# Strassen's seven products in the down projection of a transformer block, from the second super chunk on

## The chip, the cores and the metric

The kernel runs on one core of a Trainium2 chip. The core has TensorE (PE, matrix products into PSUM banks), VectorE (DVE), ScalarE (ACT) and GpSimd (POOL) for element-wise work, and SyncE (SP), which here only issues DMA transfers. Each engine works through its own list of instructions in order; semaphores tie the lists together. The metric is the device time of one execution in microseconds (us), the median of several runs. Before the change it is 2608.47 us (three runs, 2606.03 to 2609.94).

## What is computed

A transformer block on one sequence of 2048 tokens, width 576, all in float32:

```python
h  = x + attention(layernorm(x), wqkv, wo)      # 32 heads of 18
g  = layernorm(h) @ w_gate                      # 576 x 4608
u  = layernorm(h) @ w_up                        # 576 x 4608
h2 = h + (gelu(g) * u) @ w_down                 # 4608 x 576
```

The change touches the last line only: the product with `w_down` (the down product) and how its left factor, gelu(g) * u, is handed over.

## The kernel before

Float32 accuracy comes from pairs of float16: each factor is cut into a high part and a low part (value less high part), and a product of two factors is three float16 matmuls (high x high, high x low, low x high) added up in PSUM.

The feed-forward part runs from about 1392 us to the end. The 4608 hidden columns are cut into 18 chunks `c` of 256, two chunks make a super chunk `sc` (nine in all). The tokens are cut into four blocks of 512, two blocks make a pair `p`. For one super chunk the order of work is: unit(c, 0) and unit(c+1, 0), down(0), unit(c, 1) and unit(c+1, 1), down(1). The down product of pair 0 of super chunk `sc+1` stands at the end of the loop body of `sc` (L1364 to L1391).

**unit(c, p)** (L1111 to L1200) makes gelu(g) * u for 256 hidden columns and 1024 tokens. Gate and up products are done by a Strassen scheme in seven products each, so that a unit has 14 products of seven matmuls (L1125). The products go by turns into six PSUM banks, `g[0..2]` and `u[0..2]`. A bank is used several times in a unit: the first, fifth, ninth and eleventh product all add into `g[0]` (the second, sixth, tenth and twelfth into `u[0]`), and between two of them ACT copies the sum so far into a temporary (L1143, L1158, L1171 for `g[0]`; L1146, L1162, L1175 for `u[0]`). DVE adds the other banks to the temporaries (L1149, L1153, L1172, L1177, L1192, L1196), ACT applies gelu (L1130), DVE multiplies by u (`gate`, L1133). The result is four blocks of 128 hidden columns by 512 tokens, made one after the other in the temporaries xg, bg, ga and ag. Each is cut: `high` is a cast to float16 on ACT (L1136), `low` is a subtraction on POOL (L1139). The last one, ag, is ready only after the fourteenth product: addition L1196, gate L1133, high, low.

**down(p, dsc)** (L1202 to L1219) multiplies the result with `w_down`: eight row blocks of 128 tokens, two column halves of 288, each a group of 12 matmuls of 128x288 (four hidden blocks of 128, three matmuls each; issued from L300) in one of four banks. DVE multiplies a finished bank with the scale and adds it to `nat`, the residual rows in SBUF (L1215). `nat` holds all 2048 rows (16 tiles of 576 columns) throughout; after the last super chunk the rows are stored to the output (L1219).

**Side work.** Weights for the next super chunk are prepared beside these products, in steps: a generator yields after each step, and `take` runs one step of it after a product of the main work. What a step issues stands in the engines' lists at that place. `split_matrix` (L982 to L1035) is one such generator, made four times a super chunk: g2, u2, g3, u3 (gate and up matrices of the next two chunks). It makes four block sums on POOL (L993), takes the largest magnitude (`exponents`, L129 to L146: DVE reductions, a small transpose on PE, a few small DVE operations), and then cuts the matrix, in three steps each with an ACT high part (L1013) and two DVE low parts (L1027, L1029). With its `then` it has the next matrix loaded over SP (L977, L979). `split_down` (L1080 to L1105) is the last: two reductions, the small chain that gives the scale `p_s_dn`, and then four pieces, ACT high (L1096, L1100) and DVE low (L1101), into `dh` and `dl`. The order of the side steps is written in the driver:

```python
side = chain(g2, pause(2), u2, pause(2), g3, pause(2), u3, pause(4), dn)
beside(islice(u := unit(c + 1, 1), 13), side)
run(u)
beside(down(1, dsc, last), side, head=2)
```

`beside` takes one side step after each product of the main work (after `head` of them). The lists of PE, DVE, ACT, POOL and SP all have the written order (`manual_schedule`).

## Time and profile before

| what | value |
|---|---|
| runs | 2606.03, 2608.47, 2609.94 us; median 2608.47 |
| profiled execution, span | 2604.1 us |
| TensorE busy | 2579.3 us, 99% |
| DVE / ACT / POOL busy | 2010.0 / 1661.3 / 818.9 us |
| down products (L300, 128x288) | 3456 matmuls |
| unit products (L1125, 128x512) | 3528 matmuls |
| moved by DMA | 118.23 MB |

The profile is of one execution. Its page gives each engine's busy time, groups of equal instructions with their count, total and mean time, and the idle time before them with what ended it. The chain of waits goes back from the last instruction to what released each step: what stands on it sets the end. A timeline lists single instructions: start, length, engine, line, operation, tile written <- tiles read, and in brackets the idle time before it. A view by windows gives each engine's busy time within a stretch: PE, weight loads, DVE, ACT, POOL, then the granted clock. Names such as `p_s_m` are the program's tiles; `bank` and `more` are PSUM banks. For matmuls the length of one contains its way through the array, so the pace is read from the starts.

### The profile page before, as it was taken

The page shows a single profiled execution, that of the slowest core. Times are in us where ns is not written, and L with a number is a line of the kernel's source. Part 1 is how long each engine was busy: PE and PEld are TensorE (multiplying, and loading weights), DVE is VectorE, ACT ScalarE, POOL GpSimd, SP SyncE. Part 2 cuts the span into 40 slices and gives each one's busy share as a digit, 9 for nine tenths or more (in the row PEclk, how much of TensorE's full clock was granted, in tenths as well). Part 3 has the DMA queues.
Part 4 walks back from the last instruction along what each step waited for, and adds up shares of the span by engine and source line. Part 5 has one row for each costly group of instructions (what it writes and reads, how often), then busy time and mean ns, then how long its engine had stood idle before and what let it go on. Part 6 is the DMA issues. An engine that isn't in the chain of part 4 may idle for free.

```text
span 2604.1 us, 53642 instructions
## 1 busy us (share of the span) xinstructions
PE 2579.3 (99%) x20765; PEld 1198.2 (46%) x20765; DVE 2010.0 (77%) x3886; ACT 1661.3 (64%) x3124; POOL 818.9 (31%) x1146
## 2 busy tenths in 40 slices
PE   8999999999999999999999999999999999999999
PEld 4543333333333333333335555555555555555555
DVE  8479999999999999999867675757565656565653
ACT  6229999999999999999774543424243433333332
POOL 4302532322223232324585432323232323222221
PEclk9999999999999999999999999999999999999999
DMA  8621010101001010101135410101010101010110
GB/s 227 154 77 45 17 47 17 44 19 39 20 23 41 16 43 16 47 16 32 38 64 116 83 34 30 34 30 34 30 34 30 34 30 34 30 34 30 34 56 37
DMA packets 170193, 118.23 MB, mean 45 GB/s; under 512 B 88664, under 2 KB 147564, under 8 KB 169938
## 3 DMA queue, kind: packets, MB, share of 16 engines
q1 hardware_dynamic: 161198, 98.47, 14.2%
q0 software_dynamic: 8608, 16.33, 2.6%
q8 instruction: 162, 2.65, 0.4%
q14 instruction: 93, 0.76, 0.1%
q10 hardware_dynamic: 132, 0.01, 0.0%
HBM read 80.05 MB, written 15.01 MB: 37 GB/s over the span
## 4 chain that ended last, share of the span: by engine, by line
PE 92%; DVE 4%; POOL 1%; DMA 1%; issue 1%; ACT 1%; SPq 0%; POOLq 0%; ACTq 0%
PE bank L673 19%; PE bank L1125 15%; PE more L1125 15%; PE bank L300 11%; PE more L300 8%; PE quad L615 7%; PE bank L615 6%; PE quad L300 4%; PE quad L665 4%; DVE mx L625 3%; PE bank L665 3%; DVE nat L688 1%; DMA A<-qk_hi 0%; POOL A L1055 0%; ACT A L155 0%
## 5 line engine op out<-in xcount | busy, mean ns | idle before, releaser
L667 ACT ACTIVATE WK<-quad 128x512 f32<-128x512 f32 x1170 | 656.2, 621 | 23.4 <-PE quad L665 21.0
L673 PE MATMUL bank<-WK,V 128*32 128x256 f32 x8192 | 606.6, 388 | 2.7 <-DVE nat L688 0.6
L625 DVE TENSOR_REDUCE mx<-quad 128x1 f32<-128x512 f32 x836 | 553.8, 684 | 9.0 <-PE quad L665 1.5
L667 ACT ACTIVATE WK<-bank 128x512 f32<-128x512 f32 x878 | 504.9, 622 | 11.1 <-PE bank L665 9.3
L625 DVE TENSOR_REDUCE mx<-bank 128x1 f32<-128x512 f32 x716 | 477.1, 684 | 33.5 <-PE bank L615 26.4
L300 PEld LDWEIGHTS <-WK 128*128 128x128 f16 x3456 | 338.2, 98 | 88.3
L1125 PEld LDWEIGHTS <-W 128*128 128x128 f16 x2394 | 234.3, 98 | 278.3
L673 PEld LDWEIGHTS bank<-WK,V 128*32 128x32 f32 x8192 | 190.0, 108 | 268.2 <-issue 201.3
L300 PE MATMUL more<-W,WK 128*128 128x288 f16 x1728 | 235.2, 286 | 0.0
L300 PE MATMUL bank<-W,WK 128*128 128x288 f16 x1728 | 235.2, 286 | 0.0
L698 POOL TENSOR_TENSOR rp<-rc,minus_one 128x4 f32<-128x4 f32 x112 | 111.2, 1012 | 383.9 <-DMA rc<-nat 383.9
L1125 PE MATMUL bank<-X,W 128*128 128x512 f16 x792 | 223.8, 379 | 0.0
L1125 PE MATMUL bank<-V,W 128*128 128x512 f16 x720 | 202.4, 379 | 0.0
L993 POOL TENSOR_TENSOR A<-A 128x384 f32<-128x384 f32 x136 | 138.1, 1036 | 200.2 <-DMA A<-in_B_w_up_dram 83.7
L615 PE MATMUL quad<-W 54*128 54x512 f16 x514 | 191.0, 382 | 0.2 <-DVE mx L625 0.2
L615 PEld LDWEIGHTS <-W 54*128 54x128 f16 x1024 | 74.5, 94 | 241.3 <-issue 226.8
L1139 POOL TENSOR_TENSOR WK<-tmp,WK 128x512 f16<-128x512 f32 x73 | 88.5, 1212 | 305.8 <-ACT WK L1136 305.6
L615 PEld LDWEIGHTS <-A 54*128 54x128 f16 x1024 | 71.1, 94 | 231.0 <-issue 216.7
L1143 ACT COPY tmp<-more 128x512 f32<-128x512 f32 x36 | 20.9, 582 | 238.3 <-PE more L1125 203.4
L665 PE MATMUL quad<-A 56*128 56x512 f16 x584 | 172.1, 380 | 0.3
L615 PE MATMUL quad<-A 54*128 54x512 f16 x462 | 171.6, 382 | 0.1
L665 PE MATMUL quad<-W 56*128 56x512 f16 x586 | 167.5, 380 | 0.1
(348 smaller groups left out, 4122.3 us busy)
## 6 DMA issues: line engine op xcount, KB each, us to landing
A<-in_B_w_down_dram SPq DMA_DIRECT2D x8, 1152.0 KB
nat<-rc SPq DMA_DIRECT2D x32, 256.0 KB
A<-in_B_w_gate_dram SPq DMA_DIRECT2D x64, 128.0 KB
A<-in_B_w_up_dram SPq DMA_DIRECT2D x64, 128.0 KB
qk_hi<-tmp SPq DMA_DIRECT2D x36, 128.0 KB
qk_lo<-tmp SPq DMA_DIRECT2D x36, 128.0 KB
out_dram<-nat SPq DMA_DIRECT2D x16, 288.0 KB
X<-nat SPq DMA_DIRECT2D x100, 36.0 KB
```

Of the source, the lines that this page charges most:

```text
L300: nc.tensor.matmul(dst, a, b, start=(i == 0), stop=(i == len(pairs) - 1))
L615: nc.tensor.matmul(pm[:, :TB], Q[r, q0 : q0 + P], keys, start=True, stop=True)
L625: nc.vector.tensor_reduce(dst, pm[:, :TB], axis=AX.X, op=ALU.max)
L665: nc.tensor.matmul(pS[:, :TB], K[r, kt * P : (kt + 1) * P], Q[r, qc * TB : (qc + 1) * TB], start=True, stop=True)
L667: nc.scalar.activation(pes[(2 * kt + hh // 2) % NPE][:, hh % 2], pS[:, :TB], AF.Exp, scale=ex_reg)
L673: nc.tensor.matmul(acc[32 * hh : 32 * hh + 32, qs], Vg[n // NB][:, kt * G4 + hh * VC : kt * G4 + hh * VC + 32], pes[(2 * kt + hh // 2) % N ...
L688: (nc.scalar.copy if n >= NS - 2 else nc.vector.tensor_copy)(oT, acc[:, :TB])
L698: nc.gpsimd.tensor_tensor(rc[:, c : c + 4], den[:, c : c + 4], minus_one.to_broadcast([P, 4]), op=ALU.pow)
L993: op(W8[:, d], W8[:, a], W8[:, b])
L1125: nc.tensor.matmul(bank, w, x_, start=start and i == 0, stop=i == len(mm) - 1, skip_group_check=not start)
L1139: nc.gpsimd.tensor_sub(hl[:, 2 * i + j], v, hh[:, 2 * i + j])
L1143: nc.scalar.copy(xg, g[0])
```

## The change

From the second super chunk on, the down product of one super chunk and one pair, a 2 x 2 block product (two hidden halves, two blocks of tokens against two column halves), is done by Strassen's scheme with seven block products in place of eight. This needs sums of the factors:

- `unit`, for c >= 2, makes seven left factors in place of four: A11 (bg), A12 (ag), A22 (xg), and HS1 = ga + xg, HS2 = HS1 - bg, HS3 = bg - ga, HS4 = ag - HS2. The sums are four added DVE operations; seven highs on ACT and seven lows on POOL take the place of four each. Five of the seven lows now stand at the end of the unit.
- `split_down7` takes the place of `split_down`: it scales `w_down` on ACT in place (two 128x1152), forms four sums on POOL (128x576), and cuts seven parts, each an ACT copy and a DVE subtraction (128x576). The POOL memset of `blank_rows` ends it, as before.
- `down7` takes the place of `down`: for two row tiles at a time seven products of six matmuls, two of them at a time by turns in six banks, which are the banks of `unit`. Three of the seven add on to the sum that a former one left in its bank, after DVE has added that sum to the rows. DVE has 24 additions of 128x288 and 4 of twice 288 in a call. In `down7(1)` a side step is taken after every second product, from the third on.
- The seven right factors lie where `nat` had the rows of pair 1. So only one pair's rows are in SBUF: as rows are done they are stored to `nat_d` in DRAM (in the last super chunk to the output), and after the products the other pair's rows are loaded. The first super chunk keeps `down` and stores pair 1's rows.
- One temporary moves and one is added; pause(4) becomes pause(2); scale constants change.

The core of the diff:

```diff
+    def split_down7(sc):
+        df = view(A, W8O, (4, D))
+        ed = yield from exponents([view(A, W8O + 4 * 2 * D * i, (1, 2 * D)) for i in range(2)], "dn")
+        s = down_scale(ed, 266, -258)
+        B11, B12 = (df[:, 1::2, n * HALF : (n + 1) * HALF] for n in range(2))
+        B21, B22 = (df[:, ::2, n * HALF : (n + 1) * HALF] for n in range(2))
+        T3 = view(A, W8O + 4 * 4 * D, (2, HALF))
+        def part(m, v):
+            h, l = (d[:, m].rearrange("p (c n) -> p c n", c=2) for d in (dh7, dl7))
+            nc.scalar.copy(h, v)
+            nc.vector.tensor_sub(l, v, h)
+        for c in range(2):
+            nc.scalar.activation(df[:, 2 * c : 2 * c + 2], df[:, 2 * c : 2 * c + 2], AF.Copy,
+                                 scale=s[:, c : c + 1])
+        nc.gpsimd.tensor_sub(T3, B22, B12)
+        nc.gpsimd.tensor_sub(B12, B12, B11)
+        yield
+        part(HA11, B11)
+        part(HA12, B21)
+        yield
+        nc.gpsimd.tensor_sub(B11, B22, B12)
+        nc.gpsimd.tensor_sub(B21, B21, B11)
+        part(HS4, B22)
+        part(HS1, B12)
+        yield
+        part(HS3, T3)
+        part(HS2, B11)
+        yield
+        part(HA22, B21)
+        blank_rows()
+        yield
...
         gate(ga, u[0])
-        high(1, 0, ga)
-        low(1, 0, ga)
+        if seven:
+            nc.vector.tensor_add(xu, ga, xg)
...
         gelu(ag, ag)
+        if seven:
+            high(HS1, xu)
+            low(HS1, xu)
+            nc.vector.tensor_sub(bu, xu, bg)
...
         gate(ag, au)
+        if seven:
+            high(HS2, bu)
+            low(HS2, bu)
+        high(A12_, ag)
+        low(A12_, ag)
+        if seven:
+            nc.vector.tensor_sub(ga, bg, ga)
+            nc.vector.tensor_sub(au, ag, bu)
+            high(HS3, ga)
+            low(HS3, ga)
+            high(HS4, au)
+            low(HS4, au)
...
+    def down7(p, dsc, last, more):
+        Xs, Bs, Zs = ([banks[k], banks[3 + k]] for k in (1, 0, 2))
...
+        def leave(t):
+            g = 2 * p * TPB + t
+            nc.sync.dma_start(ov[:, g] if last else nat_d[:, g], nat[:, t])
+        for i0 in range(0, TPB, 2):
+            for m, bs, start, n in ((HA11, Xs, True, 0), (HA22, Bs, True, 0), (HS1, Zs, True, 1),
+                                    (HS2, Xs, False, 1), (HA12, Bs, True, 0), (HS3, Xs, False, None),
+                                    (HS4, Zs, False, 1)):
+                for k in range(2):
+                    i = i0 + k
+                    product(bs[k], m, i, start)
+                    if m == HS3:
+                        add2(bs[k], i)
+                        leave(i)
+                    else:
+                        add(bs[k], i if m in (HA22, HS1) else TPB + i, n)
+                        if m == HS4:
+                            leave(TPB + i)
+                    yield
+        if more:
+            for t in range(2 * TPB):
+                nc.sync.dma_start(nat[:, t], nat_d[:, 2 * (1 - p) * TPB + t])
...
-            side = chain(g2, pause(2), u2, pause(2), g3, pause(2), u3, pause(4), dn)
+            side = chain(g2, pause(2), u2, pause(2), g3, pause(2), u3, pause(2), dn)
...
-        beside(down(1, dsc, last), side, head=2)
+        if sc:
+            for i, _ in enumerate(down7(1, dsc, last, not last)):
+                if i >= 2 and i % 2 == 0:
+                    take(side)
+        else:
+            beside(down(1, dsc), side, head=2)
+            tmps[5] = view(nat1, 15 * 4 * D, (TB,))
+            tmps.append(view(V, 36864, (TB,)))
...
-        beside(down(0, dscs[-1], sc == NCH // 2 - 2), iter(()))
+        run(down7(0, dscs[-1], sc == NCH // 2 - 2, True))
```

More of the change, by code (lines that the diff above doesn't have):

```diff
@@ new lines, in tile_block @@
+    DT = 2 * HALF
+    dh7 = view(nat1, 8 * 4 * D, (7, DT), F16)
+    dl7 = view(nat1, 8 * 4 * D + 2 * 7 * DT, (7, DT), F16)
+    HA11, HA12, HS4, HA22, HS1, HS2, HS3 = range(7)
+    h7 = [([view(WK, 2 * TB * m, (TB,), F16) for m in range(7)],
+           [view(WK, 2 * TB * (7 + m), (TB,), F16) for m in range(7)]),
+          ([view(W, 23296 + 2 * TB * m, (TB,)) for m in range(7)],
+           [view(W, 23296 + 2 * TB * (7 + m), (TB,)) for m in range(5)]
+           + [view(WK, 2 * TB * (14 + m), (TB,), F16) for m in range(2)])]
@@ L1203, in down @@
+    def down(p, dsc):
         for j in range(2):
@@ L1359, in tile_block @@
     run(side)
-    for i, _ in enumerate(down(0, dscs[-1], NCH == 2)):
+    for i, _ in enumerate(down(0, dscs[-1])):
         take(rows, 1 + (i % 4 == 3))
```

80 lines of the change are left out of this document (52 added, 28 removed).

## Prediction

> **What bounds the kernel now.** I read the page first, then the chain of waits over the feed-forward stage, then the chain of one super chunk, and last the timelines of DVE, ACT and POOL there.
>
> ```profile
> span 2604.1 us, 53642 instructions
> PE 2579.3 (99%) x20765; PEld 1198.2 (46%) x20765; DVE 2010.0 (77%) x3886; ACT 1661.3 (64%) x3124; POOL 818.9 (31%) x1146
> ```
>
> The chain of waits from 1700 us to the end:
>
> ```profile
> by line: PE bank L1125 31.4%; PE more L1125 31.3%; PE bank L300 18.2%; PE more L300 18.2%; PE more L138 0.2%; PE bank L138 0.2%; DVE nat L1215 0.1%; issue 0.0%
> ```
>
> In this stage the set end is TensorE alone: it never waits. A matmul removed there is time saved, and any wait put there is time lost. The same chain, one super chunk (start, length, what):
>
> ```profile
> 2092.91 1.51 PE more L1125 x7
> ...
> 2114.28 1.47 PE more L300 x12
> ```
>
> A unit is fourteen products of 1.51 us (with two small transposes in this one, 21.37 us to the next start), a down call sixteen groups of 1.47 us, without a gap.
>
> **What is removed.** A down call has 16 x 12 = 192 matmuls; the new one has 4 x 7 = 28 products of 6 = 168, of the same shape. One matmul is 1.47 / 12 = 0.1225 us, a product of six 0.735 us. Saved: 24 x 0.1225 = 2.94 us a call, in 16 of the 18 calls: 47.0 us. If nothing waits, the span is 2557.1 us. Per super chunk the saving is 5.9 us, and I look for the waits that eat it: TensorE, ACT, DVE and POOL each work in written order, so a step put ahead of an operation delays it.
>
> **What hides.** Rows leave and return through SP: eight stores and eight loads of 288 KB (2.36 MB each way) a call. The next call that needs them is two units (42 us) away.
>
> ```profile
> 2090.65 0.37 SPq L1075 DMA_DIRECT2D A<-in_B_w_down_dram  x1
> ```
> ```profile
> 2095.93 2.61 DVE L129 TENSOR_REDUCE ac_dn<-A 128x1 f32<-128x1152 f32 x2 [1.43 <-DMA A<-in_B_w_down_dram]
> ```
>
> 1152 KB issued at 2090.65 were read at 2095.93, 5.3 us later, so 4.7 MB take about 22 us. SP also issues the matrix loads; those behind the row loads come half a unit later or more. I take nothing; without that cover it would be some 11 us a call for the loads. The temporaries that move, the scale constants and the shorter pause cost nothing by themselves.
>
> **Price list.** Durations of the nearest operations:
>
> ```profile
> L711 POOL TENSOR_TENSOR nat<-nat 128x512 f32<-128x512 f32 x30 | 38.3, 1276 | 189.9 <-DMA nat<-rc 119.8 <-DVE mx L625 55.3 <-DVE mx L623 7.4
> L1139 POOL TENSOR_TENSOR WK<-WK 128x512 f16<-128x512 f32 x35 | 40.5, 1157 | 96.1 <-ACT WK L1136 96.1
> L909 POOL TENSOR_TENSOR A<-A 128x288 f32<-128x288 f32 x4 | 3.2, 805 | 11.3 <-ACT A L907 11.3
> ```
> ```profile
> L248 ACT CAST A<-nat 128x576 f16<-128x576 f32 x16 | 10.0, 671 | 5.7 <-DVE nat L236 4.6 <-issue 1.0
> L1013 ACT ACTIVATE W<-A,p_s_m 128x1152 f16<-128x1152 f32 x26 | 32.6, 1255 | 119.8 <-DVE p_s_m L173 119.8
> L1175 ACT COPY tmp<-bank 128x512 f32<-128x512 f32 x35 | 20.5, 585 | 19.4 <-PE bank L1125 18.6
> ```
> ```profile
> L851 DVE TENSOR_TENSOR V<-V 128x512 f16<-128x512 f32 x2 | 1.4, 694 | 0.1
> ```
>
> From 288 to 512 columns POOL adds 0.47 us, so a 576-column subtraction is 1.4 us (an estimate; at one rate per column it would be 1.44). A `low` is 1.16 us, a part's ACT copy 0.67, a DVE subtraction 0.65.
>
> DVE and POOL also hold each other up:
>
> ```profile
> 1418.05 1.75 DVE L1027 SCALAR_TENSOR_TENSOR W<-A,p_s_m,W 128x768 f16<-128x768 f32 x1
> 1419.84 1.40 DVE L1029 SCALAR_TENSOR_TENSOR W<-A,p_s_m,W 32x384 f16<-32x384 f32 x1
> ```
> ```profile
> 1416.58 2.41 POOL L993 TENSOR_TENSOR A<-A 128x384 f32<-128x384 f32 x2
> 1418.96 1.87 POOL L1139 TENSOR_TENSOR WK<-tmp,WK 128x512 f16<-128x512 f32 x1
> ```
>
> The next rows have L1027 at 1.02 and L1029 at 0.61 undisturbed; here they took 0.73 and 0.79 more, and POOL's 1.16 became 1.87: they take turns, one whole operation each. The tail of a new unit is just such a queue: five `low`s on POOL against gate and two subtractions on DVE.
>
> **Wait A: the unit before `down7(0)`, 8 times.** `split_down7` lies there as side steps. The 26 side steps taken up to the end of `down7(1)` (13 and 13) are g2's four, a pause of two, u2's nine, two, g3's nine; the next unit takes 14: two, u3's nine, two, the first of `split_down7`. So in the unit after it the sixth step, with the scalings, stands behind the fifth product, and the seventh to ninth, a pair of parts each (last HS3 and HS2), behind the sixth to eighth: ahead of ACT's copy of the ninth product (L1171). The eleventh product adds into that bank and must wait for that copy. Today:
>
> ```profile
> 2093.75 0.75 DVE L1133 SCALAR_TENSOR_TENSOR WK<-W,p_hsc,WK 128x512 f32<-128x512 f32 x1
> ...
> 2100.81 0.42 DVE L142 TENSOR_REDUCE ab_dn<-bank 128x2 f32<-128x256 f32 x1
> ...
> 2101.92 1.01 DVE L1089 TENSOR_TENSOR M<-e_dn 128x1 int32<-128x1 int32 x1
> ...
> 2103.77 0.17 DVE L173 TENSOR_SCALAR p_s_dn<-pi_s_dn 128x2 int32<-128x2 int32 x1
> ```
> ```profile
> 2103.98 0.78 ACT L1096 ACTIVATE W<-A,p_s_dn 128x576 f16<-128x576 f32 x1 [1.16 <-DVE p_s_dn L173]
> ```
>
> The scale p_s_dn is ready at P = 11.1 us after the unit's start at 2092.91, and TensorE waits for nothing that ACT does there (the chain above). In the new kernel, from P: two scalings on ACT 2.4; then POOL T3 1.4, B12 1.4, the unit's own `low` 1.16, B11 1.4, so P + 7.8; HS2's copy 0.67 and the delayed copy 0.58: P + 9.0. The eleventh product is due at 10 x 1.51 + 0.2 = 15.3. With P = 11.1, 4.9 us are lost. But P moves: DVE ended the unit ahead at 1.5 (2093.75 + 0.75); to that come u3's last cut, now one product later (1.2, as the two rows of 2054.82 below), and four subtractions (2.6), less 0.6 that falls into gaps: 4.7. Its two-input operations take turns there with three `low`s, up to 1.16 each: 7.9. Then two reductions 2.6, two additions and a gate 2.0, the small chain 2.3 (2100.81 to 2103.94 less L1089's 0.85 of waiting), 0.2 for gelu: P = 15.0. Loss 24.0 - 15.3 = 8.7; without the turns P = 11.8 and 5.5. I take the first, since the rows at 1416 us are this very pattern. A wait of 3 us at the fifth product (ACT copies HS4 ahead of the first bank) is contained in it. 8 x 8.7 = 69.6.
>
> **Wait B: `down7(1)` with the side work, 7 times.** The tail and the additions today, in the down call that began at 2048.02:
>
> ```profile
> 2048.20 1.02 DVE L1027 SCALAR_TENSOR_TENSOR WK<-A,p_s_m,W 128x768 f16<-128x768 f32 x1 [0.73 <-ACT W L1013]
> 2049.24 0.61 DVE L1029 SCALAR_TENSOR_TENSOR W<-A,p_s_m,W 32x384 f16<-32x384 f32 x1
> 2049.89 0.69 DVE L1196 TENSOR_TENSOR W<-bank,W 128x512 f32<-128x512 f32 x1
> 2050.68 0.75 DVE L1133 SCALAR_TENSOR_TENSOR WK<-W,p_hsc,WK 128x512 f32<-128x512 f32 x1
> 2051.35 0.51 DVE L1215 SCALAR_TENSOR_TENSOR nat<-more,p_dsc,nat 128x288 f32<-128x288 f32 x1
> 2051.78 0.51 DVE L1215 SCALAR_TENSOR_TENSOR nat<-bank,p_dsc,nat 128x288 f32<-128x288 f32 x1
> ...
> 2054.82 0.74 DVE L1027 SCALAR_TENSOR_TENSOR WK<-A,p_s_m,W 128x512 f16<-128x512 f32 x1
> 2055.58 0.47 DVE L1029 SCALAR_TENSOR_TENSOR W<-A,p_s_m,W 32x256 f16<-32x256 f32 x1
> ...
> 2058.79 0.94 DVE L129 TENSOR_REDUCE ac_m<-A 128x1 f32<-128x768 f32 x1
> ```
> ```profile
> 2047.90:2071.50 23.60, 23.60 (x195) 18.88 (x194) 17.47 (x34) 6.06 (x8) 5.06 (x5) 1.00 0.13 37
> ```
>
> DVE (third busy number) already has 17.5 of 23.6 us there. An addition follows the last after 0.43 to 0.44 us. Instead of 16 there are 24 of 0.44 and 4 double ones of 0.74 (0.3 for 288 columns more): 13.5 us, in a call of 20.7. The first could start at 3.3 us today (2051.35 less 2048.02); at 5.3 with three more subtractions ahead that don't fall into the wait for ACT; at 8.4 if three `low`s take turns (3.1). HS2 adds into HA11's bank and is due at 3 x 1.47 = 4.4, so TensorE waits at once. The queue then stays behind it. Up to the first half's second double addition DVE has ten additions 4.4, two double ones 1.5, u2's last two cuts 2.4 with a `low` to wait for 1.0, the scales 0.6 (four of 0.15) and a reduction 0.95: 8.4 + 10.85 = 19.3. That addition frees the bank of the second half's second product, and TensorE has 13 products of 0.735 left from there, and a transpose of 0.1: end at 29.0 instead of 20.7. Behind it DVE's lag no longer reaches TensorE (HS2's second addition stands at 25.8, its bank is due at 26.8). Without turns: 5.3 + 9.85 = 15.2, end at 24.8. Loss 8.3; 4.1 without. 7 x 8.3 = 58.1.
>
> **Wait C: plain tails.** Before `down7(0)` gate ends at 1.5, then `low` 1.16, subtraction 0.65, `low`, subtraction: 5.1, first addition 5.5 against 4.4: 1.1, eight times, and once in the last call: 9.9. Between the units of pair 1 ACT's HS4 copy and bank copy end at 6.3 against 6.04: 0.3 x 8 = 2.4. Without turns, nothing.
>
> **Sum.** -47.0 + 69.6 + 58.1 + 9.9 + 2.4 = +93.0: span 2697.1. The median of the runs is 2608.47 - 2604.1 = 4.4 above the span, so 2701.5 us.
>
> One place more: the window above shows a granted clock of 1.00 (the number behind POOL's), and TensorE has no gap there, so the sum makes no matmul slower. By the Trainium skill, "TensorE: Matmul & The Clock Gate", Part 1, an idle window of about 3.4 us halves TensorE's clock until a busy one has passed; wait A has a gap of some 4.5 us, so an estimate by that page is one gap in three holding a whole window, each costing 2 to 3 us: 5 to 8 us more, 2707 to 2710. No row here shows such a gap; at even odds it stays inside the forecast's case.
>
> **Rivals.**
> 1. The waits come, but POOL's turns cost DVE little, because the `low`s are late themselves: A 4.9 to 5.5, B 4.1, C nothing. -47 + 8 x 5.5 + 7 x 4.1 = +26 (2634); with P = 11.1 +21 (2629). For it: no L1215 row was stretched, and turns are rare today. Against it: L1027 and L1029 above.
> 2. Faster: ACT's queue doesn't hold the eleventh product. That needs the copy by 15.3, so P + 9.0 <= 15.3 or parts that run behind the copy. With B spread by the side's gaps too, 2561; with A at P = 9.9 (the fourth product ends at 6.2, addition, gate and small chain 3.7, nothing late) and no B, -47 + 8 x 3.6 = -18: 2590. The point at which it decides is 5.9 us of waiting a super chunk. Against it: ACT alone has 7.0 us from P to the copy, and P can't precede the fourth product.
> 3. The interleaved views of one buffer are held to overlap, so that ACT's parts wait for POOL's in-place sums one after the other: the copy at about P + 13.5, 4.5 us more in A, 8 x 4.5 = 36: 2737. Nothing in this trace shows such views.
>
> **Chances.** Forecast 0.48, rival 1 0.24, rival 2 0.14, rival 3 or longer 0.09; 0.05 that waits and saving meet within 0.2% (5 us, about what a measurement of this kernel can tell from no change). Slower 0.81, same 0.05, faster 0.14. Range 2600 to 2745: it leaves out rival 2 and a few in a hundred above rival 3. For the slower cases alone 2629 to 2737.
>
> **What would show it.** TensorE's share falls from 99% to about 95%, with 384 matmuls fewer. The waits should name ACT's copy of the ninth product before a unit product (about 8 of them, 4 to 5 us each) and `nat` additions before `down7` products. In `down7(1)` DVE should be busy throughout, with HS2 and HS3 products starting late; `down7(0)` should take about 21.7 us, `down7(1)` about 29. Wrong: if the stage shows TensorE with no waits (then rival 2), if the wait sits on rows landing from DRAM, or if DVE's subtractions stay at 0.7 beside POOL's `low`s (then rival 1).

## The result and the profile after

The changed kernel takes 2758.32 us (median of four runs, 2754.67 to 2758.85), the kernel before 2608.88 (four runs): a ratio of 1.0572, 95% interval 1.0559 to 1.0585. It is 149.4 us slower; 93.0 were forecast, and 2758 lies 13 us above the range.

The page of the changed kernel:

```profile
span 2757.0 us, 54241 instructions
...
PE 2594.8 (94%) x20381; PEld 1174.7 (43%) x20381; DVE 2321.2 (84%) x4230; ACT 1740.0 (63%) x3260; POOL 1034.9 (38%) x1274
```

The 384 matmuls are gone (20765 to 20381), and TensorE's share fell from 99% to 94%. DVE has 311 us more, POOL 216 more. The chain of waits over the same stretch as before, from 1700 us to the end:

```profile
by line: PE more L1175 14.9%; PE bank L1175 13.5%; PE more L1286 10.2%; PE bank L1286 10.0%; issue 9.1%; DMA A<-in_B_w_up_dram 2.1%; DVE tmp L1183 2.1%; DVE W L1029 2.1%; DVE nat L1291 1.9%; DVE W L1027 1.7%; DVE V L1183 1.7%; DVE tmp L1267
```

TensorE held all but 1% of this chain before; now its two kinds of product (L1175 units, L1286 `down7`) hold 49%, and DVE's lines stand among them. ("issue" is time in which an engine waited for nothing that the profile shows; the view breaks the line off at its end.) What TensorE waited for in the feed-forward stage, from 1390 us (sum, times, longest):

```profile
PE more L1286 <- DVE nat L1291: 48.6, 23, 3.1
PE more L138 <- DVE am_dn L133: 20.7, 4, 5.2
PE bank L138 <- DVE am_dn L133: 19.8, 4, 5.2
PE more L1175 <- ACT nat L1226: 16.9, 4, 5.9
PE more L1175 <- ACT tmp L1226: 14.2, 4, 4.2
PE more L1175 <- ACT V L1198: 4.3, 8, 0.5
```

Line 1 is the additions of `down7`, lines 4 and 5 ACT's copy of the ninth product: both were forecast. Lines 2 and 3 were not forecast: the transposes of `w_down`'s maxima stand in TensorE's list, and TensorE stops at them.

From the starts of TensorE's stages in both traces, summed over all super chunks in which the scheme runs:

| stage | times | before, us | forecast change | measured change |
|---|---|---|---|---|
| unit pair ahead of `down7(0)` | 8 | 341.0 | +69.6 | +109.2 |
| `down7(0)` | 8 | 188.2 | -23.5 + 8.8 = -14.7 | -5.9 |
| unit pair ahead of `down7(1)` | 8 | 339.9 | +2.4 | +14.3 |
| `down7(1)` with side work | 7 | 165.4 | -20.6 + 58.1 = +37.5 | +31.6 |
| the last `down7(1)`, to the end of the span | 1 | 27.3 | -2.9 + 1.1 = -1.8 | -0.8 |
| sum (of the unrounded times) | | | +93.0 | +148.2 |

The other 4.6 us of the difference of the spans (152.8) lie ahead of the first of these stages, which began that much later in this execution.

**One unit ahead of `down7(0)`.** It starts at 2175.03 and takes 34.44 us instead of 21.37. TensorE:

```profile
2179.56 1.68 PE L1175 MATMUL bank<-X,W 128*128 128x512 f16 x7
2186.41 0.69 PE L138 MATMUL bank<-id,am_dn 128*128 128x128 f32 x2 [5.18 <-DVE am_dn L133]
2186.89 3.19 PE L1175 MATMUL more<-V,W 128*128 128x512 f16 x7
2189.88 2.66 PE L1175 MATMUL bank<-V,W 128*128 128x512 f16 x7
...
2201.75 2.83 PE L1175 MATMUL more<-V,W 128*128 128x512 f16 x7 [3.16 <-ACT nat L1226]
2204.36 2.25 PE L1175 MATMUL bank<-V,W 128*128 128x512 f16 x7
```

Two stops, in brackets, and behind each the next two products take 3.0 and 2.5, or 2.6 and 2.1 us from start to start, where 1.51 is usual. DVE at the tail of the unit ahead, and the parts:

```profile
2178.78 1.74 DVE L1183 SCALAR_TENSOR_TENSOR WK<-nat,p_hsc,WK 128x512 f32<-128x512 f32 x1
2180.45 1.64 DVE L1266 TENSOR_TENSOR tmp<-A,tmp 128x512 f32<-128x512 f32 x1
2182.01 1.64 DVE L1267 TENSOR_TENSOR nat<-WK,V 128x512 f32<-128x512 f32 x1
2183.57 2.60 DVE L129 TENSOR_REDUCE ac_dn<-A 128x1 f32<-128x1152 f32 x2
...
2190.66 0.17 DVE L173 TENSOR_SCALAR p_s_dn<-pi_s_dn 128x2 int32<-128x2 int32 x1
2194.66 9.01 DVE L1133 TENSOR_TENSOR nat<-A,nat 128x576 f16<-128x576 f32 x6 [3.82 <-ACT nat L1132]
```

The gate and the two subtractions take turns with POOL's `low`s (1.6 to 1.7 us each), as forecast. The scale is ready at 2190.83, P = 15.8 (forecast 15.0). POOL's sums and the unit's own `low` behind it, and the end of ACT's line:

```profile
2193.71 1.41 POOL L1138 TENSOR_TENSOR A<-A 128x576 f32<-128x576 f32 x1 [7.94 <-issue]
2195.20 1.80 POOL L1139 TENSOR_TENSOR A<-A 128x576 f32<-128x576 f32 x1
2196.97 1.67 POOL L1194 TENSOR_TENSOR W<-tmp,W 128x512 f16<-128x512 f32 x1
2198.60 1.91 POOL L1144 TENSOR_TENSOR A<-A 128x576 f32<-128x576 f32 x1
```
```profile
2200.54 0.67 ACT L1132 CAST nat<-A 128x576 f16<-128x576 f32 x1 [2.26 <-POOL A L1144]
2201.12 0.58 ACT L1226 COPY nat<-more 128x512 f32<-128x512 f32 x1
```

The copy ends at 2201.70, P + 10.9, where P + 9.0 was forecast.

**One `down7(1)`**, from 2125.54: DVE's tail and first addition, TensorE's two long stops, and the window of the stage.

```profile
2130.13 1.64 DVE L1266 TENSOR_TENSOR tmp<-V,tmp 128x512 f32<-128x512 f32 x1
2131.69 1.64 DVE L1267 TENSOR_TENSOR A<-nat,tmp 128x512 f32<-128x512 f32 x1
2133.26 0.51 DVE L1291 SCALAR_TENSOR_TENSOR nat<-more,p_dsc,nat 128x288 f32<-128x288 f32 x1
```
```profile
2133.81 0.88 PE L1286 MATMUL more<-nat,WK 128*128 128x288 f16 x3 [3.08 <-DVE nat L1291]
2140.43 0.53 PE L1286 MATMUL more<-nat,WK 128*128 128x288 f16 x3 [1.85 <-DVE nat L1291]
```
```profile
2125.54:2153.77 28.23, 22.85 (x171) 17.21 (x170) 26.81 (x48) 9.32 (x12) 11.71 (x10) 0.94 0.20 69
```

The first addition starts 7.7 us in (forecast 8.4), HS2 stops for it, HS3 stops later; DVE is busy for 26.8 of 28.2 us, and the stage lasts 28.2 (forecast 29.0).

### The profile page after: what moved, and what is told of

The parts are those of the page before. It is cut to its first block, busy times and chain, and to the rows that moved or that the text cites. A ratio compares the mean times of both kernels' runs of the same rounds, so it can differ in the third digit from the quotient of the medians.

```text
span 2757.0 us, 54241 instructions
## 1 busy us (share of the span) xinstructions
PE 2594.8 (94%) x20381; PEld 1174.7 (43%) x20381; DVE 2321.2 (84%) x4230; ACT 1740.0 (63%) x3260; POOL 1034.9 (38%) x1274
## 3 DMA queue, kind: packets, MB, share of 16 engines
q1 hardware_dynamic: 195758, 169.27, 20.6%
## 4 chain that ended last, share of the span: by engine, by line
PE 70%; DVE 16%; issue 5%; ACT 3%; DMA 2%; POOL 2%; SPq 1%; DVEq 0%; ACTq 0%; POOLq 0%
PE bank L673 18%; PE more L1175 8%; PE bank L1175 7%; PE quad L615 7%; PE bank L615 6%; PE more L1286 4%; PE bank L1286 4%; PE quad L300 4%; PE quad L665 4%; PE bank L300 4%; PE bank L665 3%; DVE mx L625 3%; PE more L300 1%; DMA A<-in_B_w_up_dram 1%; DVE W L1029 1%
## 5 line engine op out<-in xcount | busy, mean ns | idle before, releaser
L667 ACT ACTIVATE WK<-quad 128x512 f32<-128x512 f32 x1170 | 656.3, 621 | 26.0 <-PE quad L665 23.6
L625 DVE TENSOR_REDUCE mx<-bank 128x1 f32<-128x512 f32 x716 | 477.3, 685 | 35.5 <-PE bank L615 26.8
L1175 PEld LDWEIGHTS <-W 128*128 128x128 f16 x2394 | 242.6, 101 | 341.4 <-issue 85.5
L1175 PE MATMUL bank<-X,W 128*128 128x512 f16 x792 | 225.3, 382 | 0.0
L1175 PE MATMUL bank<-V,W 128*128 128x512 f16 x720 | 212.3, 395 | 0.5 <-ACT WK L1217 0.5
L1286 PEld LDWEIGHTS <-WK 128*128 128x128 f16 x1472 | 147.3, 100 | 97.1 <-issue 54.2
L1286 PE MATMUL more<-nat,WK 128*128 128x288 f16 x736 | 142.4, 294 | 48.6 <-DVE nat L1291 48.6
L1013 ACT ACTIVATE W<-A,p_s_m 128x768 f16<-128x768 f32 (+1 forms) x78 | 79.0, 1036 | 149.1 <-DVE p_s_m L173 149.1
L1175 PE MATMUL more<-V,W 128*128 128x512 f16 x414 | 125.3, 439 | 36.0 <-ACT nat L1226 16.9
L615 PE MATMUL bank<-A 54*128 54x512 f16 x442 | 152.3, 383 | 1.9 <-DMA A<-qk_hi 1.8
```

What stands on the lines that cost most here:

```text
L615: nc.tensor.matmul(pm[:, :TB], Q[r, q0 : q0 + P], keys, start=True, stop=True)
L625: nc.vector.tensor_reduce(dst, pm[:, :TB], axis=AX.X, op=ALU.max)
L667: nc.scalar.activation(pes[(2 * kt + hh // 2) % NPE][:, hh % 2], pS[:, :TB], AF.Exp, scale=ex_reg)
L1013: by = hi_on or (lambda dst, src, k: nc.scalar.activation(dst, src, AF.Copy, scale=k))
L1175: nc.tensor.matmul(bank, w, x_, start=start and i == 0, stop=i == len(mm) - 1, skip_group_check=not start)
L1286: nc.tensor.matmul(bank[:, :HALF], a, b, start=start and k == 0, stop=k == len(mm) - 1, skip_group_check=not start)
```

## The experiments

Stage times below are means over the super chunks from the third on unless said otherwise (the other pair without the last one, `down7(1)` over its seven calls with side work); "pair" is the unit pair ahead of `down7(0)`. Each experiment was run twice; a trace is of one execution. In the changed kernel: pair 56.0, `down7(0)` 22.9, other pair 44.4, `down7(1)` 28.1; before: 42.6, 23.5, 42.5, 23.6.

**1. Without the tail's lows.** Theory 1 was that of the prediction: turns of DVE and POOL, and ACT's line. Theory 2: the rows that go to DRAM and back.

```diff
             high(HS1, xu)
-            low(HS1, xu)
+            if c < 4:
+                low(HS1, xu)
```

(and so for HS2, A12, HS3 and HS4.)

> Leaves out the five low subtractions at the end of a unit (HS1, HS2, HA12, HS3, HS4) from the third super chunk on, so POOL has nothing to do there; the low parts used are those of the second super chunk. Theory 1 (the queues: turns of DVE and POOL in the tail, ACT held behind the parts, DVE overfull in down7(1)): down7(1) from 28.1 to about 24.8 us in six calls (-20), down7(0) from 22.6 to 20.7 in seven (-13), the units of pair 0 some 4 to 5 us shorter a super chunk (-32), those of pair 1 1 us (-7): 2686 us. Theory 2 (the residual rows' way through DRAM holds up the weight loads, and those the rest): no change, 2750 to 2765.

2693.9 us, 8 above what theory 1 gave: the pair fell by 2.8 us (to 52.3 to 53.9) where 4 to 5 were expected. Further, `down7(0)` fell to 20.6 to 21.2, the other pair to 42.5, `down7(1)` to 25.0 to 25.3 but for one of 26.7. Five POOL operations a unit are worth 64 us, though POOL is busy for less than half of the time: the two subtractions at the end of the unit (L1266, L1267) fall from a median of 1.64 us to 0.68. Waits of TensorE for a `low` itself were only 3.4 us in the changed kernel. Rival 1 ("turns cost DVE little") falls. Without the lows the scheme is still 85 us slower than before.

**2. Without the rows' traffic.**

```diff
-            nc.sync.dma_start(ov[:, g] if last else nat_d[:, g], nat[:, t])
+            if last:
+                nc.sync.dma_start(ov[:, g], nat[:, t])
...
-                nc.sync.dma_start(nat[:, t], nat_d[:, 2 * (1 - p) * TPB + t])
```

> Leaves out the stores of residual rows to DRAM between super chunks and their loads (71 MB), so the sums of the two pairs run together; all else as after. Theory 1 (queues): 2750 to 2762 us, every stage as long as before. Theory 2 (row traffic): most of the 149 us comes back, 2620 to 2690.

2760.7: nothing. Theory 2 falls, and the prediction's nothing for the transfers was right.

**3. `split_down7` three products later.**

```diff
-            side = chain(g2, pause(2), u2, pause(2), g3, pause(2), u3, pause(2), dn)
+            side = chain(g2, pause(2), u2, pause(2), g3, pause(2), u3, pause(5), dn)
```

> The pause ahead of the down matrix's preparation is 5 steps in place of 2, nothing else: the transposes stand behind the seventh product in place of the fourth, the parts behind ACT's copy of the ninth product. Theory 1: TensorE's wait of 5.2 us at the transposes goes, the wait for the copy shrinks to some 3 to 4 us; a unit pair of pair 0 from 55.7 to about 47 us, in all 2680 to 2700 us. Theory 2 (row traffic): no change by more than 10 us.

2744.4, a miss by 44. The pair lost 6.6 us (to 49.4) and the stop at the transposes was gone, but two others came up. In the pair the fifth product now stops for 3.6 us (for ACT's copy of the first bank, L1198), which the prediction had named as contained in wait A. And `down7(0)` grew by 5.6 to 28.5, where TensorE now waited for parts (DVE L1133, 2.9 us each time) and for lows. The stop had only moved: the parts had no room behind them.

**4. TensorE kept busy in its gaps.** Idle matmuls ahead of the transposes (14), of the eleventh product (9), and of the first HS2 of `down7(1)` (9).

```diff
+            fill_pe(14)
         pt = next(m_ring)
...
+        if seven and p == 0 and c % 2:
+            fill_pe(9)
         product(0, g[0], A22, T4, False)
```

> After, with idle matmuls of 128x512 in TensorE's queue ahead of its long waits (14 before the down matrix's transposes, 9 before the eleventh product there, 9 before HS2's first product in down7(1)): they add nothing to what is waited for, but shorten the gaps to about 2 us. If the matmuls after a gap are slow because the gap is long (clock halved), they come back to full pace: 1.7 us in a unit of pair 0 and 1.4 us in down7(1), 8 x 1.7 + 7 x 1.4 = 23: 2735 us. If their slowness has another cause, 2758 or a little more.

2759.4. The pair lost 1.6 us (to 54.1 to 54.3, once 55.4), with a granted clock of 0.97 where it was 0.91. `down7(1)` stayed at 28.1 to 28.2 in three cases and took 29.6 to 31.1 in four, for a cause that was not looked for, so nothing was won in all. The slow pace is on the path in the pair. In `down7(1)` it costs nothing: in the changed kernel the call that began at 2427.92 had the same stop of 3.07 us at HS2, but a granted clock of 1.00, and took 28.1 us like the others (28.0 to 28.2 at 0.88 to 0.94); the three filled calls of 28.1 to 28.2 had 1.00 as well.

**5. What a stop costs by itself.** In the kernel before, seven stops of set length in `down(0)`, one in each of seven super chunks, so that each length stands once.

```diff
+    def gap(n):
+        pd = next(m_ring)
+        t = small.tile([P, 1], F32, tag="gap", name="gap")
+        nc.tensor.matmul(pd[:, :512], id16, XT[:, 0, :512], start=True, stop=True)
+        nc.scalar.copy(t, pd[:, :1])
+        for _ in range(n):
+            nc.scalar.copy(t, t)
+        nc.tensor.transpose(pd[:, :P], t.to_broadcast([P, P]), id32)
```

> The kernel before with one stop of TensorE of a set length in down(0) of seven super chunks: a product into a spare bank, a chain of 2, 4, 7, 10, 13, 17 and 23 small copies on ACT, and a transposition that reads the last. At an estimated 0.2 us a copy the stops are about 0.6 to 5 us, some 17 us in all. Theory 1 (a stop also halves the clock behind it): from about 3 us of stop on, the six matmuls of the products behind it run at half pace for 1.5 to 3 us, so the stages with the three longest stops grow by the stop and 1.5 to 2 us more, those with the short ones by the stop alone: 2630 to 2634. Theory 2 (only the stop itself is lost): every stage grows by its stop, 2625 to 2628.

2635.6, 1.6 above the range of theory 1. By stage:

| stop shown, us | 0.47 | 0.92 | 1.59 | 2.26 | 2.93 | 3.82 | 5.16 |
|---|---|---|---|---|---|---|---|
| stage longer by, us | 1.01 | 1.46 | 2.13 | 2.80 | 4.90 | 6.03 | 8.18 |
| beyond stop and 0.54 for its own matmuls | 0 | 0 | 0 | 0 | 1.4 | 1.7 | 2.5 |

The fourth and the fifth stop, and TensorE behind them:

```profile
2132.83 0.32 PE L1350 MATMUL bank<-id,gap 128*128 128x128 f32 x1 [2.26 <-ACT gap L1349]
2132.99 1.63 PE L300 MATMUL more<-W,WK 128*128 128x288 f16 x12
...
2268.59 0.47 PE L1350 MATMUL bank<-id,gap 128*128 128x128 f32 x1 [2.93 <-ACT gap L1349]
2268.86 2.96 PE L300 MATMUL more<-W,WK 128*128 128x288 f16 x12
2271.66 1.63 PE L300 MATMUL bank<-W,WK 128*128 128x288 f16 x12
```

Twelve matmuls that take 1.47 us from start to start take 2.80 behind the stop of 2.93. So theory 1 holds: the three longest stops cost themselves and 1.4 to 2.5 us more, the four shorter ones only themselves.

The length alone does not decide it. The granted clock changes in steps of 3.41 us that lie on a fixed grid: in this trace halved steps begin at 2268.15, 2408.10 and 2544.63, 41 and 40 steps apart. The steps around the fourth stop (the first two lines) and the fifth (first number TensorE's busy time, third from the end the granted clock):

```profile
2128.20:2131.61 3.41, 2.37 (x19) 1.57 (x17) 1.04 (x2) 0.88 (x5) 2.60 (x3) 1.00 0.00 0
2131.61:2135.03 3.42, 2.20 (x18) 1.80 (x19) 0.37 (x1) 1.01 (x6) 0.00 (x0) 1.00 0.00 0
2264.74:2268.15 3.41, 0.93 (x7) 0.42 (x5) 0.52 (x1) 2.10 (x12) 0.90 (x1) 1.00 0.00 0
2268.15:2271.56 3.41, 2.96 (x13) 1.93 (x14) 0.00 (x0) 0.36 (x2) 0.00 (x0) 0.50 0.02 5
```

The grid cuts the stop of 2.26 us into 1.04 and 1.22; of the stop of 2.93 us 2.48 fall into one step, and the next step is granted half. In the traces of all runs here, from 1400 us on, each of the 278 full-clock steps in which TensorE was idle for more than 2.1 us was followed by a half one, and none of the 6680 with less than 1.5 us. So for a stop of 2.1 to 3.5 us (the longest one here that no half step followed) it depends on where the grid cuts it: the stop of 3.07 us at 2433.16 in the changed kernel lies in two steps with 1.5 and 2.0 us idle, and no slow pace follows.

**6 and 7. DVE in POOL's place.** First the four sums of `split_down7` on DVE, then the tail's five lows as well.

```diff
-        nc.gpsimd.tensor_sub(T3, B22, B12)
-        nc.gpsimd.tensor_sub(B12, B12, B11)
+        nc.vector.tensor_sub(T3, B22, B12)
+        nc.vector.tensor_sub(B12, B12, B11)
```

> The changed kernel with the four sums of w_down's parts on DVE instead of POOL. Theory 1 (turns, and ACT's copy in line behind parts that wait for POOL): a sum takes about 0.75 on DVE against 1.4 to 1.9 on POOL, the parts' subtractions fall from 1.44 to about 0.8, the copy of the ninth product comes at 6 us behind the scale instead of 10.9, the 3.2 us wait of the eleventh product and the 1.7 of slow pace behind it go: 4 to 5 us in each super chunk, 2718 to 2730. Theory 2 (DVE's load is the limit, wherever it waits): 2.8 us more on DVE, the wait comes back in down7(0) as it did with the later split: 2750 to 2770.

> As the kernel with the sums on DVE, and also the five low parts of each unit's tail on DVE. Theory 1 (turns): three of DVE's tail operations fall from 1.64 to 0.69, which pays for most of five subtractions of about 0.69; no low waits for POOL. The unit pairs ahead of down7(1) fall from 44.4 to 43, down7(1) from 28.1 to 27, the other pair as in the kernel with the sums alone: 2695 to 2720. Theory 2 (load): 13.8 us more on DVE in each super chunk less about 9 of turns; down7(1) 29 or more, 2755 to 2790.

The sums alone: 2724.2, as theory 1 had it; pair 50.7, `down7(0)` 23.7. The parts' subtraction by its own line, shortest, median and longest in ns, in the changed kernel and with the sums on DVE:

```profile
L1133 DVE TENSOR_TENSOR nat<-A,nat x56: 741/1705/1966, 1588.5 to 2657.7; 128x576 f16<-128x576 f32 x56
```
```profile
L1133 DVE TENSOR_TENSOR nat<-A,nat x56: 744/750/1621, 1587.9 to 2626.0; 128x576 f16<-128x576 f32 x56
```

DVE got 32 operations more and was busy for 19 us less (2302.5 against 2321.2), since so much less took turns with it. With the lows as well: 2812.2, slower as theory 2 had it, by 22 us more than its range. `down7(0)` took about 30.5, `down7(1)` 30.5: five subtractions more stand ahead of the first additions there. The same cure is right where POOL delays a chain and wrong where DVE's own line is the chain.

**8. 2.7 us more on DVE, stage by stage.**

```diff
+    def extra(n):
+        for _ in range(n):
+            nc.vector.tensor_reduce(small.tile([P, 1], F32, tag="xt", name="xt"), XT[:, 0, :512],
+                                    axis=AX.X, op=ALU.max)
```

> The changed kernel with four reductions of 0.68 us more on DVE (2.7 us) in one stage: in the second unit ahead of down7(1) in super chunks 2 and 6, in the middle of down7(1) in 3 and 7, at the start of the second unit of the other pair in 4, in the middle of down7(0) in 5. Theory 1 (DVE is the limit from down7(1) to the parts of w_down, and has room elsewhere): 0 in 2 and 6, 2.7 in 3 and 7, 2 to 3 in 4, 0 to 1 in 5: 2765 to 2769 in all. Theory 2 (the waits are latencies of ACT, POOL and the clock, and DVE's load has room everywhere): under 1 in each, 2758 to 2761.

2765.7, inside theory 1's sum, but not by its parts: +3.0 in the pair, +1.1 twice in `down7(1)`, +0.8 twice in the other pair, one of them with 2.2 more in the `down7(1)` behind it; `down7(0)` took 24.5, as it does now and then without. Only the pair passes on all of it. Inconclusive for `down7(1)`.

**9 to 12. The tail later, alone and with the sums on DVE.** The last two subtractions of a unit and the highs and lows of HS3 and HS4 are issued behind the fourth product of the next unit, or in `down7` ahead of the first HS1.

```diff
-        if seven:
+        def tail():
             nc.vector.tensor_sub(ga, bg, ga)
             nc.vector.tensor_sub(au, ag, bu)
...
+        if seven:
+            later.append(tail)
         yield
...
+                    if m == HS1 and k == 0:
+                        flush()
                     product(bs[k], m, i, start)
```

> The changed kernel with the last two subtractions of a unit's tail and their four highs and lows (HS3, HS4) issued later: behind the fourth product of the next unit of the pair, or in down7 behind the adds of its first four products. Theory 1 (the order of DVE's queue makes part B and the transposes' wait): the first add of down7(1) comes 3.3 us earlier, the 3.08 and most of the 1.85 us stop and their slow pace go, down7(1) 28.1 to 25.5-26.5; the reductions of w_down start 3.2 us earlier, the pair ahead of down7(0) 55.7 to 52-53; 2710 to 2725. Theory 2 (DVE's load in these stages is the limit, 26.8 of 28.2 us in down7(1)): the stops move to later products of down7, 27.5 or more; the pair 54 to 55.7; 2745 to 2760.

> Both: the later tail and the four sums of w_down's parts on DVE, which alone gave 2724.2 with 50.7 in the pair ahead of down7(0) and 23.7 in down7(0). Theory 1: pair 46 to 48, down7(0) 22.5 to 24, down7(1) 25.5 to 26.5: 2670 to 2695. Theory 2: pair 49 to 50.7, down7(1) 27.5 or more: 2710 to 2724.

> As the kernel with both, and w_down's reduction, transposes and parts one product later (pause of 3 instead of 2). Theory 1 (with the parts' chain shorter by 5 us there is room behind it): the rest of the transposes' wait shrinks by 1.5, down7(0) as without it: 2660 to 2685. Theory 2 (every product later comes back in down7(0)): the same as without it within 5.

> As the kernel with both, and w_down's part two products later (pause of 4). Theory 1: no stop at the transposes left, pair 43.5 to 45, down7(0) at most 1 more: 2650 to 2680. Theory 2: down7(0) grows by what the pair loses, 25 to 27: the same within 8 of the kernel with a pause of 2.

| kernel | us | pair | `down7(0)` | other pair | `down7(1)` |
|---|---|---|---|---|---|
| tail later | 2735.6 | 55.9 | 20.8 | 42.7 | 29.0 |
| and sums on DVE | 2704.7 | 52.4 | 21.5 | 42.7 | 28.6 |
| and pause(3) | 2701.6 | 51.7 | 22.1 | 42.7 | 28.7 |
| and pause(4) | 2699.6 | 50.4 | 23.1 | 42.7 | 28.8 |

The first two totals lie between the theories, the last two where theory 2 had them. What was forecast as wait C is gone (the other pair at 42.7 in all four, `down7(0)` at 20.8 with the tail later alone). But `down7(1)` did not fall, against theory 1, and in the pair with the tail later alone the transposes stop 2.6 us instead of 5.2, while the eleventh product now stops 5.8: the same copy, no earlier. With each later start the pair loses what `down7(0)` gains, but for a few tenths. `down7(1)` in the last of them, additions and the cuts of u2's side steps on DVE, and TensorE's stop:

```profile
2098.57 1.48 DVE L1027 SCALAR_TENSOR_TENSOR WK<-A,p_s_m,W 128x512 f16<-128x512 f32 x1
...
2102.64 1.48 DVE L1027 SCALAR_TENSOR_TENSOR WK<-A,p_s_m,W 128x512 f16<-128x512 f32 x1
2104.14 1.27 DVE L1029 SCALAR_TENSOR_TENSOR W<-A,p_s_m,W 32x256 f16<-32x256 f32 x1
2105.44 0.52 DVE L1301 SCALAR_TENSOR_TENSOR nat<-bank,p_dsc,nat 128x288 f32<-128x288 f32 x1
```
```profile
2106.44 0.88 PE L1296 MATMUL more<-nat,WK 128*128 128x288 f16 x3 [4.39 <-DVE nat L1301]
```

The first addition now comes 4.3 us in instead of 7.7, but the moved lows on POOL meet the cuts on DVE (0.74 and 0.48 undisturbed), and the stop stands at HS3 with 4.4 us.

**13 to 16. Copies ahead of the parts, side steps late.** Is the rest the order in which ACT and DVE take their work, or DVE's load? For the pair: scaling two products later, parts and products of `down7(0)` in the order HA11, HS1, HA12, HS2, HA22, HS3, HS4. For `down7(1)`: its 13 side steps in the second half.

```diff
-                if i >= 2 and i % 2 == 0:
-                    take(side)
+                if i >= 14 and i % 2 == 0:
+                    take(side, 2 if i < 26 else 1)
```

> The later tail, the sums on DVE and a pause of 4 (2699.6 with them, 50.0 to 51.0 in the pair ahead of down7(0), 22.6 to 23.5 in down7(0)), and w_down's scaling two products later still, so that ACT's copies of the ninth and tenth product are issued ahead of it; parts made in the order in which down7(0) now takes its products (HA11, HS1, HA12, HS2, HA22, HS3, HS4). Theory 1 (the 4.3 to 5.5 us stop of the eleventh product is ACT's order alone): pair 44 to 46, down7(0) 23 to 25.5: 2655 to 2680. Theory 2 (DVE's work from down7(1) on is the limit, wherever the stop falls): down7(0) grows by what the pair loses, 27 to 29: 2690 to 2705.

> The later tail and the sums on DVE (2704.7, down7(1) 28.2 to 29.0), and the 13 side steps of down7(1) in its second half, two at a time. Theory 1 (the stop of 4.4 us in the first half is the splitting steps between the adds): the first half runs with stops under 1 us, down7(1) 23 to 25, the pair behind it up to 2 more: 2675 to 2692. Theory 2 (DVE's load): the stops come in the second half or in the pair, and down7(1) and the pair keep their sum of 80: 2698 to 2710.

> The copies first and the side steps late together. Theory 1: the sum of both gains, 2625 to 2660, still slower than the kernel before. Theory 2: 2685 to 2705.

> As the kernel with both, with w_down's reduction and transposes two products earlier (pause of 2) and three products between them and the scaling, so that the scaling comes one product earlier. Theory 1: within 10 of the kernel with both, the transposes wait up to 2.5 us, down7(0) starts with its parts ready: 2625 to 2665. Theory 2: 2685 to 2710.

| kernel | us | pair | `down7(0)` | `down7(1)` |
|---|---|---|---|---|
| copies first | 2727.0 | 45.5 | 31.5 | 28.6 |
| side steps late | 2677.7 | 52.6 | 21.5 | 24.6 |
| both | 2703.5 | 46.0 | 31.7 | 24.5 |
| both, earlier reductions | 2707.0 | 48.3 | 29.2 | 24.6 |

Side steps late: theory 1, 4 us a super chunk, nothing given back in the pair. Copies first: the pair fell by 5, as theory 1 had it, and `down7(0)` grew by 8, more than theory 2 had; the total is 22 us above the range of either. The last two came where theory 2 had them. There one wait did it, in all eight calls:

```profile
PE more L1297 <- DVE V L1258: 38.1, 8, 5.0
```

L1258 is the unit's own last addition but one, queued on DVE behind the parts. Whichever of parts and unit goes first, the other is late. The product order was changed with it, so this run does not give the price of the order of ACT alone.

**17. No parts at all**, on top of the kernel with the side steps late.

```diff
+        if sc >= 3:
+            yield from pause(4)
+            blank_rows()
+            yield
+            return
         for c in range(2):
             nc.scalar.activation(df[:, 2 * c : 2 * c + 2], df[:, 2 * c : 2 * c + 2], AF.Copy,
```

> The kernel with the later tail, the sums on DVE and the side steps late (2677.7: pair ahead of down7(0) 51.5 to 53.7, down7(0) 20.6 to 21.8), with the scaling, the sums and the seven parts of w_down left out from the fourth super chunk on (six of eight; down7 goes on with the parts of the third, so the output is not the reference's); the reductions and transposes stay. Theory 1 (the parts' chain, scaling on ACT, sums and lows on DVE between the copy of the ninth product and the eleventh, is all that is left of A but the transposes): pair 44 to 46, down7(0) 20.6: 2628 to 2640. Theory 2 (the tail and the splitting of w_up and w_gate fill DVE without the parts): pair 48 or more: 2648 to 2665.

2642.7, nearer to theory 1: pair 46.9 in the six super chunks, `down7(0)` 20.6. What stays in the pair is a stop of 2.4 to 2.7 us at the transposes and the pace behind it. A super chunk is 46.9 + 20.6 + 42.7 + 24.9 = 135.1 us, against 132.3 before: even for nothing, the parts would not have made the scheme pay in this order of work. `down7(1)` and the pair here, windows as above (third busy number DVE):

```profile
2079.47:2104.31 24.84, 21.51 (x170) 16.31 (x169) 23.99 (x46) 7.32 (x10) 10.75 (x9) 1.00 0.23 78
2104.31:2150.18 45.87, 43.06 (x202) 19.39 (x200) 38.22 (x68) 21.49 (x35) 15.35 (x14) 1.00 0.41 135
```

DVE is busy for 62.2 of 70.7 us. A whole super chunk, before and after the change:

```profile
2137.64:2269.94 132.30, 132.30 (x784) 76.72 (x782) 82.10 (x160) 48.47 (x72) 35.59 (x33) 1.00 0.11 32
```
```profile
2125.54:2277.00 151.46, 134.27 (x738) 73.90 (x737) 122.44 (x205) 58.25 (x90) 63.08 (x50) 0.95 0.27 90
```

DVE's 82.1 us have become 122.4.

**18. Side steps late, alone.**

> The changed kernel with nothing but the 13 side steps of down7(1) moved to its second half, two at a time; the tail and the sums as the change has them. Theory 1 (the unit's tail ahead of the first adds, and the splitting steps between the adds, each make a stop of its own, so that it takes both): the 3.08 us stop of HS2 stays, the 1.85 us one goes, down7(1) 25.5 to 27 against 28.1 in the changed kernel and 24.6 with both mended: 2735 to 2750. Theory 2 (the splitting steps are all of it): 24 to 25, 2725 to 2735.

2770.7, slower than either theory: `down7(1)` 29.7. HS2 still stops (3.06 us) and the pace behind it is slow; the side steps seem to meet the late additions in the second half. Tail later alone 29.0, side steps late alone 29.7, both 24.6: either repair by itself only hands the stop on.

No version beat the kernel before; the best of those that compute the whole product, at 2677.7, is slower by a ratio of 1.0267 (1.0237 to 1.0297).

## Why the prediction was right about the sign and wrong about the size

**Right.** The saving of 2.94 us a call is there: with the tail later, five of the eight calls of `down7(0)` take 20.58, and 23.52 - 2.94 = 20.58. The transfers cost nothing. The three waits came, at the named places and for the named reasons, and the turns of DVE and POOL are real (experiment 1). B was sized within 6 us of 58.

Behind the turns stands a rule of the Trainium skill, "SBUF — State Buffer", section "Who interferes with whom": a DVE instruction with two SBUF inputs contends with a GpSimd instruction that reads SBUF, and whoever is first has the port for the whole instruction; one with at most one SBUF input outside the two-port modes does not contend. The trace agrees: the additions of `down7`, with one input in PSUM, never take longer than 0.52 us in 384 cases, 128 of which run wholly beside an operation of POOL, while a subtraction of two SBUF tiles takes 1.64 in 31 of 32, and 0.68 in the other (shortest, median, longest in ns; two groups of each):

```profile
L1291 DVE SCALAR_TENSOR_TENSOR nat<-more,p_dsc,nat x192: 501/509/520, 1610.7 to 2752.3; 128x288 f32<-128x288 f32 x192
L1291 DVE SCALAR_TENSOR_TENSOR nat<-bank,p_dsc,nat x192: 501/517/520, 1611.1 to 2753.0; 128x288 f32<-128x288 f32 x192
```
```profile
L1266 DVE TENSOR_TENSOR tmp<-A,tmp x4: 684/1636/1640, 1574.3 to 2482.7; 128x512 f32<-128x512 f32 x4
L1266 DVE TENSOR_TENSOR V<-nat,V x4: 1640/1641/1647, 1607.6 to 2514.9; 128x512 f32<-128x512 f32 x4
```

**Wrong: wait A, 69.6 forecast, 109.2 measured.** The step that failed is "then POOL T3 1.4, B12 1.4, the unit's own `low` 1.16, B11 1.4, so P + 7.8". The prediction let the turns lengthen DVE's operations and left POOL's at their undisturbed price, though the parts' subtractions run beside them. They took 1.41, 1.80, 1.67 and 1.91, and with the waits between them P + 9.7: 1.9 us, 1.4 of it the longer operations. Putting the sums on DVE, where each takes 0.75 us, gave the pair 5.3 us back, and `down7(0)` took 0.9 of them. P itself was 0.8 late. The third piece is the pace: behind the eleventh product's stop 1.7 us are lost in the unit shown, which the prediction left out of its sum ("so the sum makes no matmul slower"); filling the gaps won back 1.6. Over all eight pairs P came 6.9 us late, the way from P to the end of the copy was 16.2 us longer, and the eleventh and twelfth product lost 16.3 (1.4 to 2.9 each): 39 of the 40 us. The first pair (58.3 us) is the longest because its copy ends at P + 12.7 instead of 10.9; why, was not looked for. The stop at the transposes, which no sentence of the prediction had, costs no time of its own here: the copy is later still. It came to set the time as soon as the copy came earlier, in experiments 6 and 17, where it is the longest stop left in the pair.

**Wrong: wait C, 12.3 forecast, 34 measured.** (-5.9 + 23.5 = 17.6 in `down7(0)`, 14.3 in the other pair, -0.8 + 2.9 = 2.1 in the last call.) The step was "gate ends at 1.5, then `low` 1.16, subtraction 0.65, `low`, subtraction: 5.1", and 0.3 for the other pair. The gate takes turns too (1.74), and each subtraction takes 1.64. Moving the tail removed both waits, which shows that they were the tail's.

**The slow pace.** By the Trainium skill, "TensorE: Matmul & The Clock Gate", Part 1, an idle window of about 3.4 us halves TensorE's clock until a busy one has passed; the prediction put 5 to 8 us on it in a sentence beside the sum. The trace agrees on the halving (0.50 in the steps concerned, which makes 0.91 over the pair and 0.94 over `down7(1)`), but not on the length: stops of 3.08 and 3.16 us, and one of 2.93 in experiment 5, are followed by half pace, and a step of 3.41 us with 2.48 idle is enough. There each of the three longest stops cost 1.4 to 2.5 us more. Behind the eleventh product's stop in the eight pairs it is the 16.3 us above.

**B, and why it could not be mended at one place.** The queue was as forecast (first addition at 7.7 for 8.4, end at 28.2 for 29.0). Its two causes hide each other: additions late by the tail, and cuts of the side work between the additions. The prediction had both in one chain. The tail later alone (29.0) and the side steps late alone (29.7) do not shorten the call, both together do (24.6); that run also had the sums on DVE, which with the tail later left it at 28.6.

What stays open: how much of A is the order of ACT's list alone, since the run that put the copies first also changed the order of the products; why `down7(1)` with the side steps late alone is slower than with nothing moved; and why four calls of `down7(1)` grew when TensorE's gaps were filled.

## What to carry to other kernels

A scheme with fewer products pays with element-wise work, and that has to fit on the engines beside TensorE in the stage where it falls: here 384 of 20765 matmuls were bought with 49% more busy time on DVE (82 to 122 us a super chunk, the turns with POOL included), and the lists of DVE and ACT set the end where TensorE alone did before. When two engines take turns, price both sides of it: the operation that waits and the operation that it waits for. And a repair that moves a stop is tried together with what stands next in line; a single one only handed the stop on in experiments 3, 9, 13 and 18.

## What the runs showed of the hardware that was not expected

TensorE's clock is granted in steps of 3.41 us on a fixed grid, and a step with more than 2.1 us idle was followed by a half one in all 278 cases (experiment 5). So the slow stretch need not begin at the end of the stop: behind the stop of 3.82 us, which the grid cut into 1.81 and 2.01, the first twelve matmuls took 1.68 us from start to start, the next twelve 2.88, for the half step began only at 2408.10, 1.2 us after they set out.

Operations on two to four columns can take turns like large ones: in the kernel with pause(4), three of the small steps of the scale (L144, L146, L1101), 0.15 to 0.17 us otherwise, took 0.94, 1.08 and 1.01 beside POOL's lows, 2.5 us in all.
